# One multiply of the VectorE exponential handed to GpSimd in a conformer block, with the whole order planned again

## The chip, the cores and the metric

The kernel runs on one core of a Trainium2 chip. A core has five engines that run side by side, each with its own fixed list of instructions, and that wait for each other by semaphores: TensorE (PE in the profile; its weight loads are listed apart as PEld), VectorE (DVE), ScalarE (ACT), GpSimd (POOL) and SyncE (SP, which here only issues transfers). Data lie in SBUF, or in PSUM, where TensorE writes. The metric is the device time of one execution in microseconds; before the change it is 914.84 us (median of 3 runs, 914.69 to 915.0).

## The reference, cut to what matters

A conformer block on x of shape (2, 4000, 144) in bf16: a feed-forward layer, self-attention over 4000 tokens with 4 heads of 36, a gated convolution of width 5, a second feed-forward layer and a last normalization.

```python
h = _layernorm(x);  h = _silu(h @ w_ff1a) @ w_ff1b;  x = x + 0.5 * h
h = _layernorm(x);  qkv = h @ w_qkv                      # q, k, v: (2, 4, 4000, 36)
scores = jnp.einsum('bhqd,bhkd->bhqk', q, k) * Dh ** (-0.5)
p = _softmax(scores, axis=-1)
att = jnp.einsum('bhqk,bhkd->bhqd', p, v)
x = x + att @ w_o
h = _layernorm(x) @ w_pw1;  h = a * _sigmoid(b)          # a, b: the halves of h
c = sum over i of hp[:, i:i + T, :] * dw[i]              # hp: h padded by 2 at both ends
x = x + _silu(c) @ w_pw2
h = _layernorm(x);  h = _silu(h @ w_ff2a) @ w_ff2b;  x = x + 0.5 * h
return _layernorm(x)
```

The exponentials of the softmax are 2 x 4 x 4000 x 4000 = 128 million numbers, and they set the size of the work.

## The kernel before, in words

**Tiles.** The 8000 tokens are 16 chunks of 500 queries (8 for each batch). For one chunk the keys are taken 64 at a time: 62 full tiles and a rest of 32 keys. A tile is a pair of PSUM banks of 128 x 500: four matmuls of a 64-row corner of the array give the scores of 64 keys, 500 queries and 4 heads (`scores`, called by `emit_S`; in the profile PS<-QT,KT). The exponentials of a tile are written as bf16 to one of 11 buffers PT (128 x 1000), and four matmuls of PT against the values VA add them to the chunk's output in the two last banks (`emit_O` and `o_quads`; PS<-PT,VA). A column of ones among the values gives the softmax's sum.

**Two ways to an exponential.** Most tiles go to ScalarE: one ACTIVATE with Exp over both banks (`emit_exp`; ACT PT<-PS 128x1000). 167 of them go to VectorE (`dve_tile`, lines 1385 to 1416). The scores are scaled so that adding a bias and rounding to a 16-bit integer gives the bits of a bf16 power of two with a linear mantissa. VectorE does, for each tile z:

1. twice `tensor_scalar` from a PSUM bank to int16 in z (DVE PT<-PS, 128x500); each one gives a bank back,
2. `tensor_scalar` on the bits of z: the mantissa alone, put between a half and one, into a second buffer y (DVE PT<-PT, uint16),
3. `tensor_tensor`: y = z * y in bf16 (DVE PT<-PT, 128x1000 bf16; line 1409),
4. `tensor_scalar` on the bits of z in place: the exponent alone (DVE PT<-PT, uint16); it must come after step 3, which reads z.

y and z are both handed to the output matmuls, so that such a tile costs PE eight of them and not four.

**Other work.** While the attention runs, the layers before it for later chunks (`pre`) and those after it for earlier chunks (`post1`, `post2`) are done in the gaps of all engines. Normalization (`ln`, lines 704 to 743): VectorE takes the statistics (ST), GpSimd computes the variance's inverse root with a power (RS<-RS,NHALF) and, outside the first and last part of the run, also the mean with its sign (RS<-ST) and four normalizing steps per chunk (XN<-X,RS, 125x144). GpSimd also copies the columns at the edge of a chunk for the convolution (U<-U).

**What sets the order.** Nothing is decided on the chip. `Rec` records every operation, keeps an estimated time for each engine (`R.free`), and at the end writes each engine's list with the semaphores needed (`replay`; all instructions are issued on its line 170, so in the profile all have line 170 and are told apart by their tiles). `Rec.op` reckons an operation's start from its engine, its operands and `cost`, for instance `c_act(n)`, `c_dve(n, rate)`, XN_COST, and SWITCH for a change of the kind of matmul on PE. Background work is written as generators that say what they need next (`need`). `pick_any` chooses the next one by estimated times and by rules with numbers from the tables POLICY, TJ and FJ; POLICY has one entry per 21 tiles of the attention. `due` decides if the next tile goes to VectorE: not more than LIVE such tiles at once, DGAP us at least between two, and only if VectorE's estimated time is not later than PE's plus DSLACK. The estimate knows engines, buffers and banks; it holds an operation's cost to be the same whatever other engines do at the time. In the first part (`mode["front"]`, until the keys of the first batch are there) and in the last one other rules hold.

Of the kernel before, what the change touches and what calls it, by code (L numbers as in the profile page):

```python
# [6 lines left out]
ALU = mybir.AluOpType  # L7
# [16 lines left out]
CH = 500  # L24
# [14 lines left out]
def c_dve(n, rate=1.0):  # L39
    return n / (960 * rate) + 0.07  # L40


def c_act(n):
    return n / 1200 + 0.051
# [6 lines left out]
class Rec:  # L51
# [6 lines left out]
    SWITCH = 0.095  # L58
# [12 lines left out]
    def op(self, eng, name, *a, r=(), w=(), q=None, cost=0.1, kind=None, lat=None, **k):  # L71
        o = Op()
# [18 lines left out]
        if eng == "pe" and self.filler is not None and not self.filling:  # L91
# [5 lines left out]
            start = self.free[eng]  # L97
# [3 lines left out]
        if eng == "pe":  # L101
            if kind != self.kind:
                start += self.SWITCH
            self.kind = kind
# [147 lines left out]
class Thread:  # L252
    def __init__(self, gen, ready, rank, no=0):
        self.no = no
        self.gen, self.ready, self.live, self.rank = gen, ready, True, rank
        self.req = None
# [67 lines left out]
def bass_standalone__conformer_family_zipformer__speech_kernel(  # L324
# [28 lines left out]
    def sb(name, shape, dt=BF16):  # L353
# [7 lines left out]
        0.0, -0.6, 0, 0.0, -0.3, 0.0, 0.0, 0.0, 0.0, -0.6, 0.15, 0.15, -0.6, 0.0, 0.15, 0,  # L361
        0.0, 0.0, 0.0, 0.0, 0.0, 0.0, 0.3, 0.6, 0.6, -0.3, -0.3, 0.0, 0.0, 0.0, 0.0, 0.0,
        0.0, 0.0, 0.0, 0.15, 0.0, 0.0, 0.0, -0.15, 0.0, 0.0, 0.0, 0.0, 0, 0.6, 0.0, 0.0,
    )
    FJ = (
        0.0, 0.0, 0.0, 0.0, 0.0, 0.0, 0.0, 0.0, 0.0, 0.0, 0.0, 0.0, 0.0, 0.0, 0.0, 0.0,
        0.0, 0.0, 0.0, 0.0, 0.0, 0.0, 0.0, 0.0, 0.0, 0.0, 0.0, 0.0, 0, 0.0, 0.0, 0.0,
        -0.25, 0.0, 0.0, 0.0, 0.0, 0.0, 0.0, 0.0, 0.0, 0.0, 0, 0.0, 0.0, 0.0, 0.0, 0.0,
        0.0, 0.0, 0.0, 0.0, 0.0, 0.0, 0.0, 0.0, 0.0, 0.0, 0.0, 0.0, 0.0, 0.0, 0.0, 0.0,
    )  # L370
    FLEX = 0.3
    SEG = 21
    POLICY = {
        "AHEAD": (
            0.56, 0.56, 0.56, 0.85, 0.85, 0.85, 0.56, 0.56, 0.56, 0.56, 0.56, 0.56, 1.0, 1.0, 0.56, 0.56,
            0.56, 0.56, 0.56, 0.56, 0.56, 0.56, 0.56, 0.56, 0.56, 0.6, 0.6, 0.5, 0.5, 0.5, 0.5, 0.56,
            0.56, 0.56, 0.56, 0.56, 0.56, 0.56, 0.56, 0.56, 0.5, 0.5, 0.56, 0.56, 0.56, 0.56, 0.56, 0.56,
# [3 lines left out]
            0.4, 0.4, 0.4, 2.5, 1.5, 1.5, 1.5, 1.0, 1.0, 1.5, 0.8, 0.4, 0.4, 0.4, 0.2, 0.2,  # L381
            0.4, 0.4, 0.4, 0.4, 1.5, 1.5, 1.5, 1.5, 4.0, 4.0, 4.0, 0.4, 0.4, 0.2, 0.4, 0.4,
            0.4, 0.4, 0.4, 0.4, 0.4, 0.4, 0.2, 0.2, 0.2, 0.4, 0.4, 0.4, 0.4, 1.5, 1.5, 1.5,
# [3 lines left out]
            2.0, 2.0, 4.0, 3.5, 4.5, 4.5, 4.5, 2.5, 2.5, 2.5, 2.5, 2.5, 2.5, 2.5, 2.5, 2.5,  # L387
            2.5, 2.5, 2.5, 2.5, 4.5, 2.5, 2.5, 2.5, 2.5, 2.5, 3.0, 3.25, 3.25, 3.0, 6.0, 3.25,
            3.25, 3.25, 3.25, 3.25, 4.0, 2.5, 2.5, 2.5, 3.25, 3.25, 3.25, 4.5, 4.5, 4.5, 3.25, 3.25,
# [3 lines left out]
            3, 3, 1, 1, 4, 4, 1, 1, 1, 3, 0, 0, 0, 0, 1, 1,  # L393
            1, 1, 1, 1, 1, 1, 1, 1, 1, 1, 1, 2, 1, 1, 1, 1,
            1, 1, 1, 1, 1, 1, 0, 0, 0, 0, 0, 1, 2, 0, 0, 1,
# [3 lines left out]
            1, 1, 2, 1, 1, 1, 1, 1, 1, 1, 1, 1, 1, 1, 1, 1,  # L399
            1, 1, 1, 1, 1, 1, 1, 1, 0, 2, 2, 2, 2, 2, 2, 1,  # L400
            1, 1, 1, 1, 1, 1, 2, 1, 1, 1, 1, 1, 1, 1, 3, 2,
            2,
        ),
        "LATE": (
            0.3, 0.3, 0.3, 0.3, 0.6, 0.6, 0.1, 0.2, 0.2, 0.2, 0.2, 0.2, 0.6, 0.6, 0.6, 0.1,
            0.1, 0.1, 0.1, 0.1, 0.1, 0.3, 0.3, 0.3, 0.3, 0.3, 0.2, 0.2, 0.2, 0.3, 0.3, 0.3,
            0.3, 0.3, 0.2, 0.2, 0.2, 0.2, 0.2, 0.2, 0.2, 0.2, 0.2, 0.2, 0.2, 0.2, 0.2, 0.2,
# [3 lines left out]
            1.8, 1.8, 1.6, 1.6, 1.6, 1.6, 1.6, 2.0, 2.5, 2.5, 2.5, 2.5, 2.5, 1.4, 2.5, 2.5,  # L411
            2.5, 1.8, 2.5, 2.5, 2.5, 1.6, 1.6, 1.6, 1.6, 1.6, 1.6, 1.4, 1.4, 1.4, 1.4, 3.5,
            3.5, 3.5, 3.5, 2.5, 2.5, 1.4, 1.4, 1.4, 1.6, 1.6, 3.0, 3.0, 1.4, 1.4, 1.4, 1.8,
# [3 lines left out]
            2, 2, 2, 2, 2, 2, 2, 2, 2, 3, 3, 3, 3, 3, 2, 2,  # L417
            5, 5, 4, 2, 2, 3, 2, 2, 2, 2, 2, 2, 2, 4, 2, 4,
            4, 5, 5, 2, 2, 2, 4, 5, 5, 5, 5, 5, 5, 5, 5, 4,
            3,  # L420
        ),
        "LIVE": (
            3, 3, 2, 2, 1, 1, 1, 1, 1, 2, 2, 2, 2, 3, 3, 3,
            3, 2, 2, 2, 2, 3, 3, 2, 2, 1, 1, 2, 2, 3, 3, 3,
            3, 3, 3, 3, 3, 3, 2, 3, 3, 4, 3, 3, 3, 3, 3, 3,
# [3 lines left out]
            2, 2, 3, 3, 1, 1, 3, 2, 1, 1, 1, 1, 1, 1, 3, 2,  # L429
            3, 3, 2, 2, 1, 2, 2, 2, 2, 1, 1, 2, 2, 2, 2, 2,  # L430
            2, 2, 2, 2, 2, 2, 3, 1, 1, 1, 3, 3, 3, 3, 3, 3,
            3,
        ),
        "EARLY": (
            2, 2, 2, 1, 3, 3, 2, 2, 2, 2, 2, 2, 2, 1, 1, 1,
            2, 2, 1, 1, 2, 2, 2, 2, 2, 2, 2, 2, 2, 2, 2, 2,
            2, 1, 1, 2, 2, 2, 3, 3, 3, 3, 3, 3, 2, 2, 2, 2,
            2,
        ),
        "PW": (  # L440
            0.12, 0.12, 0.12, 0.12, 0.05, 0.05, 0.3, 0.12, 0.12, 0.05, 0.05, 0.05, 0.05, 0.05, 0.12, 0.12,
            0.12, 0.12, 0.12, 0.12, 0.12, 0.12, 0.12, 0.12, 0.12, 0.12, 0.12, 0.12, 0.2, 0.2, 0.2, 0.12,
            0.3, 0.2, 0.2, 0.2, 0.2, 0.2, 0.12, 0.12, 0.12, 0.12, 0.12, 0.12, 0.12, 0.12, 0.12, 0.12,
# [3 lines left out]
            0.1, 0.1, 0.1, 0.1, 0.1, 0.1, 0.1, 0.1, 0.1, 0.1, 0.1, 0.1, 0.1, 0.1, 0.1, 0.1,  # L447
            0.1, 0.1, 0.1, 0.1, 0.1, 0.1, 0.1, 0.1, 0.0, 0.0, 0.0, 0.1, 0.1, 0.1, 0.1, 0.1,
            0.1, 0.1, 0.1, 0.1, 0.1, 0.1, 0.1, 0.1, 0.1, 0.1, 0.1, 0.1, 0.1, 0.1, 0.1, 0.1,
            0.1,  # L450
        ),
        "BGPICK": (
            0, 0, 0, 0, 0, 0, 0, 0, 0, 0, 0, 0, 0, 0, 0, 0,
            0, 0, 0, 0, 0, 0, 0, 0, 0, 0, 0, 0, 0, 0, 0, 0,
            1, 1, 1, 0, 0, 0, 1, 0, 0, 0, 0, 0, 0, 0, 0, 0,
# [3 lines left out]
            2, 2, 2, 1, 2, 2, 2, 2, 2, 0, 0, 0, 0, 0, 2, 2,  # L459
            2, 2, 2, 2, 2, 2, 2, 2, 2, 2, 2, 2, 2, 2, 0, 0,  # L460
# [4 lines left out]
            5, 5, 5, 5, 5, 5, 5, 5, 5, 5, 5, 5, 4, 4, 4, 5,  # L465
            5, 3, 3, 3, 3, 5, 5, 5, 5, 5, 5, 5, 5, 2, 2, 5,
            5, 5, 5, 5, 5, 5, 5, 5, 5, 5, 5, 5, 5, 1, 5, 5,
            5,
        ),
        "PRELAG": (  # L470
            0.7, 0.7, 0.7, 0.7, 0.7, 1.0, 0.7, 1.5, 1.5, 0.7, 0.7, 0.7, 0.7, 0.7, 0.7, 0.7,
            0.7, 0.7, 0.7, 0.7, 0.7, 0.7, 0.7, 0.7, 0.7, 0.7, 0.7, 1.0, 1.0, 1.0, 1.0, 0.7,
            0.7, 0.5, 0.5, 0.5, 0.5, 0.5, 0.7, 0.3, 0.3, 0.3, 0.7, 0.7, 0.5, 0.5, 0.5, 0.5,
            1.0,
        ),
        "LAGD": (
            1, 1, 1, 1, 1, 1, 1, 0, 0, 0, 0, 0, 1, 1, 0, 1,
            1, 1, 1, 1, 1, 1, 1, 1, 1, 1, 1, 1, 1, 0, 0, 0,
            1, 1, 1, 1, 1, 1, 1, 1, 1, 1, 1, 0, 0, 0, 0, 1,
# [147 lines left out]
    def now(k):  # L627
        return POLICY[k][seg[0]]

# [74 lines left out]
    def ln(c, bs, e=False):  # L704
# [15 lines left out]
        if not calm:  # L720
            op("pool", "tensor_scalar", RS[0:rows, u, 2, 0:n], ST[0:rows, u, 0:n, 1], -1.0, None, op0=ALU.mult,
               r=[("MV", u)], w=[("NM", u)], cost=0.3)
            for j in range(n):
                op("pool", "tensor_scalar", XN[0:rows, u, j, :], X[0:rows, c * NB + b0 + j, :], RS[0:rows, u, 2, j:j + 1],
                   RS[0:rows, u, 0, j:j + 1], op0=ALU.add, op1=ALU.mult,
                   r=[("X", c, b0 + j), ("NM", u), ("RS", u)] + xe, w=[("XN", u)], cost=XN_COST, lat=XN_LAT)
# [18 lines left out]
    XN_COST = 0.65  # L745
    XN_LAT = 0.6
    POW_COST = 1.22
# [596 lines left out]
    def scores(n, hh, bk, cost):  # L1344
        _, c, t = its[n]
        b = c // CPB
        k0, q0 = t * KT_ROWS, c * CH
        kcs = {min(k0 // CH, CPB - 1), min((k0 + KT_ROWS - 1) // CH, CPB - 1)}
        for p in range(2):
            op("pe", "matmul", PSV[64 * p:64 * p + 64, bk, 0:CH],  # L1350
               lhsT=KT[64 * hh:64 * hh + 64, p, b, k0:k0 + KT_ROWS], rhs=QT[64 * hh:64 * hh + 64, p, q0:q0 + CH],
               start=True, stop=True, skip_group_check=True,
               r=([("WKT", 0, "a")] if b == 0 and k0 + KT_ROWS <= 2 * TB else [("WKT", b * CPB + kc) for kc in kcs])
               + [("WQT", c)], w=[("ps", bk)], cost=cost, kind="q",
               lat=0.36 if cost < 0.1 else 0.31)
# [29 lines left out]
    def dve_tile(n):  # L1385
        z = None
        for hh in range(2):
# [20 lines left out]
        yield need("dve")  # L1408
        op("dve", "tensor_tensor", yf, zf, yf, op=ALU.mult, r=[("PT", z), ("PT", y)], w=[("PT", y)],
           cost=c_dve(2 * CH, 2), kind="e")  # L1410
# [5 lines left out]
        live_dve[0] -= 1  # L1416

# [3 lines left out]
    def o_quads(m, p, cost):  # L1421
# [12 lines left out]
        for hh in range(2):  # L1434
            op("pe", "matmul", PSV[64 * hh:64 * hh + DH + 1, BX + p, 0:CH],
               lhsT=VA[64 * p:64 * p + 64, blk, hh, 0:DH + 1], rhs=PT[64 * p:64 * p + 64, pt, hh, :],
               r=[("PT", pt), ("VA", cc), "VA1"], w=[("ps", BX + p)], cost=cost, kind="q", lat=0.33, **flags)
# [86 lines left out]
    def pick_any():  # L1524
# [46 lines left out]
        if n_s[0] >= NIT and o:  # L1571
            return o[0]
        left = len(ptp.free) - owed[0]
# [132 lines left out]
```

## Time and profile before

| | |
|---|---|
| runs, median (lowest to highest) | 914.84 us (914.69 to 915.0) |
| the profiled execution | 914.9 us |
| its span, first to last instruction | 913.1 us |
| granted TensorE clock | 0.999 |
| busy: PE, DVE, ACT, POOL | 890.1, 802.0, 872.9, 277.5 us |
| first and last full exponential on ACT start | 20.6 and some 877 us |
| XN steps on GpSimd | 224, 131.8 us |
| DVE exponential tiles | 167 |

Busy time is the time in which at least one instruction of the engine runs. ACT's instructions overlap at their ends, so that the mean of one (1050 ns for an exponential) is longer than what one adds to the busy time (777.2 / 841 = 0.924 us). A wait is put down to the engine and tile that ended it. In a row of a group the last part is the idle time of the engine just before that group's instructions. PE's busy time includes the pipeline of matmuls and does not tell how full PE is; its waits do.

### The profile page before, as it was taken

To read this page: it belongs to the slowest core of one execution; us is meant where nothing else is said; L and a number is where in the kernel's file an instruction comes from. 1 tells how busy PE (TensorE), PEld (TensorE's weight loads), DVE (VectorE), ACT (ScalarE), POOL (GpSimd) and SP (SyncE) were. 2 spreads that over 40 slices of the span, in tenths; PEclk is the share of its full clock that TensorE was granted. 3 is DMA by queue.
4 is the path that set the end of the run, shared out by engine and by line. 5 is a ranking of instruction groups with operands and counts; after the bars stand their busy time and mean duration, and the time that the engine had idled before them with its cause. 6 is when DMAs were issued, how large, how long until landed. Compare 5 with 4: busy or idle time off the path is not lost.

```text
span 913.1 us, 27439 instructions
## 1 busy us (share of the span) xinstructions
PE 890.1 (97%) x11946; PEld 411.2 (45%) x11946; DVE 802.0 (88%) x1756; ACT 872.9 (96%) x1105; POOL 277.5 (30%) x519
## 2 busy tenths in 40 slices
PE   8999999999999999999999999999999999999996
PEld 7544434444444444444444444444434344444455
DVE  8988898898989999898988799897889699978987
ACT  5899999999999999999999999999999999999984
POOL 5121041145111612223415333240605050403143
PEclk9999999999999999999999999999999999999999
DMA  4000000000000000000000000000000000000000
GB/s 114 34 2 1 2 2 1 1 3 1 3 3 1 3 2 2 2 3 1 2 2 14 1 9 8 8 2 1 15 1 2 8 9 2 8 1 8 2 8 26
DMA packets 7322, 7.36 MB, mean 8 GB/s; under 512 B 2376, under 2 KB 7202, under 8 KB 7202
## 3 DMA queue, kind: packets, MB, share of 16 engines
q1 hardware_dynamic: 5786, 5.00, 1.8%
q8 instruction: 93, 1.52, 0.7%
q10 hardware_dynamic: 1416, 0.62, 0.3%
q14 instruction: 27, 0.22, 0.1%
HBM read 3.31 MB, written 2.30 MB: 6 GB/s over the span
## 4 chain that ended last, share of the span: by engine, by line
ACT 51%; PE 43%; DVE 4%; issue 1%; DMA 0%; POOL 0%; POOLq 0%; DVEq 0%
ACT PT L170 46%; PE PS L170 43%; ACT TH L170 5%; DVE HT L170 1%; DVE PT L170 1%; DVE ST L170 1%; DMA X<-in_x_dram 0%; DVE X L170 0%; DVE XN L170 0%; DVE QT L170 0%; POOL RS L170 0%; DVE XT L170 0%; DVE RS L170 0%; DVE SW L170 0%; DVE VA L170 0%
## 5 line engine op out<-in xcount | busy, mean ns | idle before, releaser
L170 ACT ACTIVATE PT<-PS 128x1000 bf16<-128x1000 f32 (+1 forms) x841 | 777.2, 1050 | 8.3 <-PE PS L170 5.9
L170 PE MATMUL PS<-QT,KT 64*64 64x500 bf16 x3968 | 415.6, 383 | 8.6 <-ACT PT L170 5.6
L170 PE MATMUL PS<-PT,VA 64*37 64x500 bf16 x4636 | 396.1, 373 | 1.9 <-DVE QT L170 1.4
L170 DVE TENSOR_SCALAR PT<-PS 128x500 int16<-128x500 f32 x334 | 222.4, 671 | 31.5 <-PE PS L170 29.5
L170 PEld LDWEIGHTS PS<-QT,KT 64*64 64x64 bf16 x3968 | 123.8, 104 | 195.7 <-ACT PT L170 112.5
L170 PEld LDWEIGHTS PS<-PT,VA 64*37 64x37 bf16 x4636 | 132.1, 95 | 111.3 <-issue 26.7
L170 POOL TENSOR_SCALAR RS<-ST 125x4 f32<-125x4 f32 x112 | 36.6, 327 | 471.0 <-DVE ST L170 465.8
L170 DVE TENSOR_SCALAR PT<-PT 128x1000 uint16<-128x1000 uint16 x334 | 134.7, 416 | 1.3
L170 POOL TENSOR_SCALAR XN<-X,RS 125x144 bf16<-125x144 bf16 x224 | 131.8, 599 | 5.8
L170 POOL TENSOR_TENSOR RS<-RS,NHALF 125x4 f32<-125x4 f32 (+2 forms) x101 | 94.1, 936 | 101.6 <-DVE RS L170 96.9
L170 DVE TENSOR_TENSOR PT<-PT 128x1000 bf16<-128x1000 bf16 x167 | 113.0, 681 | 1.5
L170 ACT ACTIVATE TH<-PS 128x500 bf16<-128x500 f32 (+3 forms) x198 | 104.3, 552 | 6.7 <-PE PS L170 5.6
L170 DVE SCALAR_TENSOR_TENSOR HT<-TH,PS 128x500 bf16<-128x500 bf16 (+1 forms) x135 | 80.6, 616 | 25.1 <-ACT TH L170 24.4
L170 PE MATMUL PS<-XT,WA 72*128 72x500 bf16 (+2 forms) x280 | 74.3, 360 | 0.6 <-DVE VA L170 0.3
L170 DVE SCALAR_TENSOR_TENSOR X<-PS,X 125x288 bf16<-125x288 f32 x128 | 57.4, 452 | 14.8 <-PE PS L170 13.1
L170 DVE BATCH_NORM_STATS2 ST<-X 125x6 f32<-125x288 bf16 (+1 forms) x160 | 65.8, 447 | 1.0 <-DMA X<-in_x_dram 0.8
L170 PE MATMUL PS<-WB,HT 128*125 128x144 bf16 (+1 forms) x640 | 52.7, 230 | 0.3 <-DVE HT L170 0.3
L170 PEld LDWEIGHTS PS<-WB,HT 128*125 128x125 bf16 (+1 forms) x640 | 44.3, 136 | 14.8 <-issue 3.8
L170 PE MATMUL PS<-IDENT,XN 125*72 125x125 bf16 x512 | 42.4, 221 | 1.5 <-DVE XN L170 0.9
L170 DVE COPY XT<-PS 72x1000 bf16<-72x1000 bf16 (+2 forms) x65 | 39.9, 617 | 3.3 <-PE PS L170 2.5
L170 PEld LDWEIGHTS PS<-IDENT,XN 125*72 125x72 bf16 x512 | 31.5, 112 | 20.2 <-issue 12.6
L170 PE MATMUL PS<-U,DG 128*128 128x250 bf16 (+5 forms) x204 | 34.3, 265 | 0.1
(86 smaller groups left out, 560.6 us busy)
## 6 DMA issues: line engine op xcount, KB each, us to landing
X<-in_x_dram SPq DMA_DIRECT2D x16, 140.6 KB
out_dram<-XN SPq DMA_DIRECT2D x14, 140.6 KB
WA<-in_w_ff1a_dram ACTq DMA_DIRECT2D x1, 144.0 KB
WB<-in_w_ff1b_dram ACTq DMA_DIRECT2D x1, 144.0 KB, 2.6
WA<-in_w_ff2a_dram SPq DMA_DIRECT2D x1, 144.0 KB
WB<-in_w_ff2b_dram SPq DMA_DIRECT2D x1, 144.0 KB
out_dram<-XN SPq DMA_DIRECT2D x2, 70.3 KB
WQKV<-in_w_qkv_dram ACTq DMA_DIRECT2D x1, 121.5 KB
```

Of the source, the lines that this page charges most:

```text
L170: ins = getattr(eng, o.name)(*o.a, **o.k)
```

## The change

In `dve_tile`, step 3 is issued on GpSimd if the plan holds it to be free early enough, and on VectorE otherwise or in the first part. G_COST is what the plan reckons for it. This comes about for 115 of now 171 tiles. Buffers and dependencies are the same: y is written by GpSimd, PE's matmuls on y and VectorE's step 4 on z wait for it.

The planner's estimates are changed in a few places: `c_act`, SWITCH, an extra time (`bub`) for the first matmul of a score or output group after a switch or a wait, and the normalizing steps on GpSimd (0.45 us each and 0.8 more for the first, in place of 0.65 each). Its rule for the next matmul can hold background work back for a while (BURST, BAGE). All tables are new, and with them the order of the instructions on every engine.

```diff
 def c_act(n):
-    return n / 1200 + 0.051
+    return n / 1200 + 0.053
...
-    SWITCH = 0.095
+    SWITCH = 0.094
...
             if kind != self.kind:
-                start += self.SWITCH
+                start += self.SWITCH + bub[0] + (0.006 if self.kind == "q" else 0.0)
+            elif start > self.free["pe"] + 0.01:
+                start += bub[1]
...
     POLICY = {
+        "PTS": (
+            0.5, 0.5, 0.5, 0.5, 0.5, 0.5, 0.5, 0.5, 0.5, 0.5, 0.5, 0.5, 0.5, 0.5, 0.5, 0.5,
...
         "DGAP": (
-            2.0, 2.0, 4.0, 3.5, 4.5, 4.5, 4.5, 2.5, 2.5, 2.5, 2.5, 2.5, 2.5, 2.5, 2.5, 2.5,
...
+            2.0, 2.0, 4.0, 3.5, 4.5, 4.5, 4.5, 4.5, 2.5, 2.5, 2.5, 2.5, 4.5, 2.5, 2.5, 2.5,
+            2.5, 2.5, 2.5, 2.5, 2.0, 2.0, 2.0, 2.0, 2.5, 2.5, 2.5, 3.0, 1.5, 1.5, 1.5, 1.5,
...
         "LIVE": (
+            3, 3, 2, 2, 2, 1, 1, 1, 1, 1, 1, 1, 1, 3, 3, 3,
+            3, 2, 3, 4, 4, 3, 1, 3, 3, 3, 3, 3, 3, 3, 3, 3,
+            3, 3, 3, 3, 3, 3, 2, 3, 3, 3, 3, 3, 3, 3, 3, 3,
             3,
         ),
...
-                   r=[("X", c, b0 + j), ("NM", u), ("RS", u)] + xe, w=[("XN", u)], cost=XN_COST, lat=XN_LAT)
+                   r=[("X", c, b0 + j), ("NM", u), ("RS", u)] + xe, w=[("XN", u)], cost=XN_COST + (j == 0) * XN_FIRST, lat=XN_LAT)
...
-    XN_COST = 0.65
+    XN_COST = 0.45
     XN_LAT = 0.6
+    XN_FIRST = 0.8
...
-        yield need("dve")
-        op("dve", "tensor_tensor", yf, zf, yf, op=ALU.mult, r=[("PT", z), ("PT", y)], w=[("PT", y)],
-           cost=c_dve(2 * CH, 2), kind="e")
+        pool = not mode["front"] and R.free["pool"] < R.free["dve"] + now("PTS")
+        yield need("pool" if pool else "dve")
+        op("pool" if pool else "dve", "tensor_tensor", yf, zf, yf, op=ALU.mult, r=[("PT", z), ("PT", y)], w=[("PT", y)],
+           cost=G_COST if pool else c_dve(2 * CH, 2), kind="e")
...
+    G_COST = 2.3
...
+        for q in ok:
+            if q[2].seen is not q[2].req:
+                q[2].seen, q[2].since = q[2].req, R.free["pe"]
+        if ok and R.kind == "q" and (s or o) and sum(q[2].req.dur for q in ok) < now("BURST") and min(
+                q[2].since for q in ok) > R.free["pe"] - now("BAGE"):
+            ok = []
```

## The prediction

> **What bounds the kernel now.** I read the page first (engine shares, then the slices, then the chain), next the busy time by stretch, the waits of the middle of the run, and last the rows of the two engines that the change touches. The profiled execution took 914.9 us, of which 913.1 is span and 1.8 lies around it; the median of the runs is 914.84, so a difference to the one is a difference to the other.
>
> ```profile
> PE 890.1 (97%) x11946; PEld 411.2 (45%) x11946; DVE 802.0 (88%) x1756; ACT 872.9 (96%) x1105; POOL 277.5 (30%) x519
> ...
> ACT 51%; PE 43%; DVE 4%; issue 1%; DMA 0%; POOL 0%; POOLq 0%; DVEq 0%
> ...
> L170 ACT ACTIVATE PT<-PS 128x1000 bf16<-128x1000 f32 (+1 forms) x841 | 777.2, 1050 | 8.3 <-PE PS L170 5.9
> L170 DVE TENSOR_SCALAR PT<-PS 128x500 int16<-128x500 f32 x334 | 222.4, 671 | 31.5 <-PE PS L170 29.5
> L170 DVE TENSOR_SCALAR PT<-PT 128x1000 uint16<-128x1000 uint16 x334 | 134.7, 416 | 1.3
> L170 POOL TENSOR_SCALAR XN<-X,RS 125x144 bf16<-125x144 bf16 x224 | 131.8, 599 | 5.8
> L170 DVE TENSOR_TENSOR PT<-PT 128x1000 bf16<-128x1000 bf16 x167 | 113.0, 681 | 1.5
> ```
>
> The chain is ACT and PE by turns; VectorE has 4% of it and GpSimd nothing. By stretch (first column the length, then PE, weight loads, DVE, ACT, POOL):
>
> ```profile
> 0.00:47.00 47.00, 43.49 (x496) 29.74 (x497) 40.83 (x125) 32.52 (x61) 15.91 (x35) 1.00 0.25 72
> 47.00:126.00 79.00, 77.89 (x1086) 32.73 (x1084) 67.18 (x172) 77.08 (x94) 12.32 (x19) 1.00 0.01 2
> 126.00:486.00 360.00, 357.20 (x4918) 158.26 (x4916) 328.83 (x676) 355.22 (x431) 111.63 (x207) 1.00 0.01 2
> 486.00:850.00 364.00, 356.24 (x4757) 156.08 (x4754) 313.88 (x643) 361.84 (x450) 118.43 (x227) 1.00 0.02 6
> ```
>
> From 126 to 850 us ACT works 717.1 of 724 us. That is the bound: only 6.9 us are left to squeeze there without taking work off ACT. It is also fragile. The waits of that same stretch:
>
> ```profile
> PEld PS L170 <- ACT PT L170: 102.8, 280, 1.1
> ...
> PEld PS L170 <- DVE PT L170: 56.0, 195, 0.6
> ```
>
> PE waits for ACT 0.37 us at a time (102.8/280); that is all the lead it has when VectorE is late. And it already waits for VectorE's exponential tiles 195 times, just in time. The order of every engine is fixed ahead, so a late VectorE instruction holds all that stands behind it.
>
> **The part that decides: two engines on one path to SBUF.** GpSimd's normalizing step XN takes 451 ns at least, 461 in the middle, but up to 2267:
>
> ```profile
> L170 POOL TENSOR_SCALAR XN<-X,RS x216: 451/461/2267, 125.8 to 846.9; 125x144 bf16<-125x144 bf16 x108
> ...
> 302.85 2.27 POOL L170 TENSOR_SCALAR XN<-X,RS 125x144 bf16<-125x144 bf16 x1
> ...
> 302.95 0.74 DVE L170 TENSOR_SCALAR PT<-PT 128x1000 uint16<-128x1000 uint16 x2
> 303.61 1.26 DVE L170 TENSOR_TENSOR PT<-PT 128x1000 bf16<-128x1000 bf16 x2
> ```
>
> The 2.27 us one stood still while VectorE ran four SBUF-to-SBUF steps on PT. Taken over the trace, the 122 XN steps that meet no PT<-PT step average 459 ns and none is over 466, whatever else VectorE does; the 102 that meet one average 768. The other way round, VectorE's PT<-PT tensor_scalar takes 410 ns where GpSimd is idle and 443 on average, 646 at most, on its 66 meetings with an XN; the multiply goes from 671 to 713 on 40 meetings, 831 at most. So the two exclude each other: here GpSimd lost 102 x 0.31 = 32 us by it, and VectorE 66 x 0.033 + 40 x 0.042 = 3.9 us, because an XN is short.
>
> **The change part by part.** *Four exponentials more leave ACT* (171 VectorE tiles for 167): 4 x 0.924 us (777.2/841) = -3.7 us on the bound. For them VectorE does 4 x (2 x 0.666 + 2 x 0.403) = 8.6 us more, without multiplies, and PE four more passes of PT against VA, 16 matmuls at 396.1/4636 = 0.085 us, 1.4 us beside ACT. *115 multiplies leave VectorE*: 115 x 0.677 = 77.9 us, on an engine that is not the bound; by itself worth nothing but the waits for it, which are limited to the 6.9 us of ACT's idle time. I count 0 and keep -4 as the end.
>
> *115 multiplies come to GpSimd.* The trace has none of this size. From RS<-ST (4 elements, 194 ns at least) and XN (144 elements, 451 ns), one element costs 257/140 = 1.84 ns, so 1000 elements cost 2.0 us with one input read and up to 3.9 us if the second is read after the first. The plan reckons with 2.3, near the lower end, where I stay. GpSimd goes from 277.5 to about 542 us, 59%. Behind a multiply stand the next normalization (56 groups) and the halo copies; PE waited on GpSimd's RS 4 times for 1.4 us in all in the middle, and GpSimd itself waits 433.9 us for ST there: background work with room, 0. If that room were gone, half of the 56 groups 1.15 us late would be 32 us on the background chain. No DMA is added, and SP's order of stores does not pass anything that matters (16 stores in all).
>
> *The added waits.* The exponent step of the same tile (z in place) may run only when GpSimd has read z, some 1.6 us later than now; the plan knows this and puts other work between. y is ready 1.6 us later, too, and PE's pass waits for it in the plan's reckoning; 11 PT buffers stay. What the plan does not know is the exclusion. In the trace 77 other-tile PT<-PT steps start within 2.3 us of the 167 multiplies (229 in all, less one own step per multiply where there is one), 0.46 each; for 115 that makes 53 meetings. A VectorE step that comes while a 2.1 us stream runs waits 1.05 us in the mean if GpSimd keeps the path for the whole stream: 56 us. If it lets go as quickly as with XN, it is 53 x 0.04 = 2 us. For XN itself the same reckoning (106 meetings, half of the time streaming, half of 0.25 us) gives 7 us where 3.9 were seen; that share makes 31 us here, 0.6 us per meeting. PE's lead hides 0.37 of each, which leaves 53 x 0.23 = 12 us. The ends are 0 and 53 x (1.05 - 0.37) = 36 us. I take 12: the row is of the same pair of engines. GpSimd's own lateness (VectorE is in PT<-PT steps for 232 of the 724 us now, 78 less then, 21%; 0.3 us for each meeting) stays under PE's 0.37.
>
> The Trainium skill (SBUF — State Buffer, Who interferes with whom) says that whoever of the two starts first keeps the shared ports for the whole instruction. The trace bears that out only in part: 33 tensor_scalar steps begin inside GpSimd's power step, which lasts 1.04 us or more, and none takes over 420 ns. With the whole 2.3 us held, a meeting would cost 1.15 us and the sum would be 53 x (1.15 - 0.37) = 41 us instead of 12.
>
> ```profile
> 279.38 1.04 POOL L170 TENSOR_TENSOR RS<-RS,NHALF 125x4 f32<-125x4 f32 x1
> ...
> 279.67 0.41 DVE L170 TENSOR_SCALAR PT<-PT 128x1000 uint16<-128x1000 uint16 x1
> ```
>
> *The new tables, the picking rule and the planner's constants* emit no instruction; they reorder all of them. Up to 126 us the multiply stays on VectorE, so only the order differs there; ACT is idle 16.4 us in that part (126 - 32.5 - 77.1) and 16 of the last 34.6 us. Either could move by a fifth, 3 us, up or down. I take 0.
>
> Sum: 914.9 - 3.7 + 12 = 923.2, rounded up for the multiplies that PE meets late: **924 us**.
>
> **The rivals.** *The relief holds (faster).* The place is VectorE's queue between 126 and 850 us: 78 us of freed time swallow the blocked steps before PE or ACT sees them, or GpSimd yields. ACT loses its four exponentials and perhaps half of its 6.9 us of idle time and a little of the ends: 914.9 - 3.7 - 3.4 = 908. For it: with 31 us of blocks against 69 us net freed, VectorE is still less loaded than now, and the trace shows GpSimd losing eight times as much as VectorE. Against: PE's lead is a third of a microsecond, and a block comes in one lump. It decides below 3.7/53 = 0.07 us lost on ACT per meeting. *The multiply is much longer than planned (slower still).* At 3.9 us, y is 1.6 us late 115 times; PE waited just in time on 195 of 616 VectorE tile events in the middle (154 tiles, two bank releases and two outputs each), so 115 x 0.32 x (1.6 - 0.37) = 45 us: 914.9 - 3.7 + 12 + 45 = 968. For it: two inputs. Against: nothing but the plan's own 2.3. *Nothing that can be told.* Blocks of 0.07 us per meeting just eat the four exponentials: 915.
>
> The Trainium skill (GPSIMD Engine Reference, Elementwise — side-by-side cycle accounting) has 4497 ns for a two-input add of 2048 elements, from which I would estimate 2.2 us; no run here shows it yet, and by it the sum above stays as it is.
>
> **How the numbers follow.** A difference under 0.2% (1.8 us) is about what a measurement of this kernel cannot tell from none. Blocks that reach ACT: 0.48, its own range 917 to 941 (1 to 26 us beyond the middle's gain). Relief holds: 0.36, 903 to 912. No difference: 0.07. Long multiply: 0.09. The range runs from 905 (leaving 0.08 of the relief's chance below) to 943 (leaving the long multiply and a little of the first case above). Faster 0.36, same 0.07, slower 0.57.
>
> **What would show it.** Right: GpSimd's multiply is a row of 115 with a middle of 2.2 to 2.6 us; PT<-PT steps on VectorE that took 410 ns now show a maximum near 2 us and a mean clearly over 443; ACT's row still ends its waits on PE PS, but its idle time from 126 to 850 us is some 15 to 25 us instead of 6.9; PE's waits on DVE PT are longer at the longest than 0.6 us. Wrong: the maximum of VectorE's PT<-PT stays under 700 ns (GpSimd yields), ACT's idle time stays under 7 us and the time falls with four full exponentials fewer (825 now, by the row of that shape); or the multiply's row is at 3 us and more, and PE waits on POOL PT. It would also be wrong if the ends of the run, outside 126 to 850 us, moved by over 3 us.

## The result and the profile after

The changed kernel takes 942.33 us (median of 4 runs, 941.25 to 942.63) against 914.82 (914.69 to 915.0): a ratio of 1.0298, with a 95% interval of 1.0281 to 1.0316. It is slower, as forecast, but by 27.5 us where 9 were forecast. The profiled execution took 942.2 us, 940.3 of them span.

The page of the changed kernel (engine shares, chain, and three groups: busy time and mean, then idle time ahead and who ended it):

```profile
PE 900.7 (96%) x11992; PEld 416.2 (44%) x11992; DVE 788.1 (84%) x1661; ACT 875.2 (93%) x1102; POOL 516.7 (55%) x640
...
PE 58%; ACT 23%; DVE 17%; issue 1%; POOL 1%; DMA 0%; ACTq 0%; DVEq 0%
...
L172 ACT ACTIVATE PT<-PS 128x1000 bf16<-128x1000 f32 x837 | 778.8, 1029 | 30.9 <-PE PS L172 26.2
...
L172 POOL TENSOR_TENSOR PT<-PT 128x1000 bf16<-128x1000 bf16 x115 | 242.9, 2113 | 236.9 <-DVE PT L172 236.8
...
L172 DVE TENSOR_SCALAR PT<-PT 128x1000 uint16<-128x1000 uint16 x342 | 171.1, 511 | 6.4 <-POOL PT L172 4.0
```

VectorE is less busy than before (788.1 us for 802.0), and yet its share of the chain has gone from 4% to 17%: it holds the others up for longer, although it is less loaded. Of the 78 us that the multiplies took off it, its bit steps on PT (the two `tensor_scalar` on the bits) took back 33 by growing from 416 to 511 ns (342 x 0.511 - 334 x 0.416 = 36, 3 of that for eight steps more). ACT's exponentials, four fewer, stood waiting for 30.9 us in place of 8.3.

By stretch (length, then PE, weight loads, DVE, ACT, POOL):

```profile
126.00:486.00 360.00, 350.29 (x4725) 154.37 (x4723) 304.63 (x596) 342.32 (x416) 212.32 (x261) 1.00 0.01 3
486.00:850.00 364.00, 348.23 (x4684) 152.64 (x4683) 307.17 (x594) 352.29 (x433) 218.52 (x249) 1.00 0.02 5
```

In these 724 us ACT works 694.6, so that it is idle 29.4 us where it was 6.9. The waits of the same stretch (total, times, longest):

```profile
PEld PS L172 <- DVE PT L172: 79.5, 206, 1.7
PEld PS L172 <- ACT PT L172: 70.1, 202, 0.8
...
ACT PT L172 <- PE PS L172: 23.0, 39, 1.9
```

PE waits for VectorE's tiles about as often as before (206 times for 195), but up to 1.7 us and not 0.6, and ACT waits for PE 23.0 us where in the kernel before it was

```profile
ACT PT L170 <- PE PS L170: 3.9, 14, 0.6
```

The rows of the instructions on PT, minimum, median and maximum in ns, tell why. On VectorE, before and after:

```profile
L170 DVE TENSOR_SCALAR PT<-PT x334: 358/410/646, 87.5 to 874.4; 128x1000 uint16<-128x1000 uint16 x167
...
L172 DVE TENSOR_SCALAR PT<-PT x342: 366/412/2279, 111.7 to 907.3; 128x1000 uint16<-128x1000 uint16 x171
```

and on GpSimd, after:

```profile
L172 POOL TENSOR_TENSOR PT<-PT x115: 2068/2078/2919, 126.4 to 905.2; 128x1000 bf16<-128x1000 bf16 x115
```

The bit step's median is what it was, its maximum 2279 ns, in place of 646. Worked out over the trace: 53 bit steps overlap a GpSimd multiply and take 1026 ns on average, 32.6 us in all above the 411 that the others take in the middle. Nearly all of this lies with 30 of them that are held, 1.09 us each: they begin inside a multiply that has more than 0.2 us to go, and every one of them ends 0.28 us (0.275 to 0.280) after it, however long that is. The 64 multiplies that meet no such step take 2.07 to 2.10 us, the 51 others 2.16 on average. So this time it is VectorE that loses. One case, from the timelines of the four engines (start, length, what, and the idle time ahead):

```profile
597.81 4.22 POOL L172 TENSOR_TENSOR PT<-PT 128x1000 bf16<-128x1000 bf16 x2 [3.54 <-DVE PT L172]
...
600.03 2.27 DVE L172 TENSOR_SCALAR PT<-PT 128x1000 uint16<-128x1000 uint16 x1 [0.53 <-POOL PT L172]
...
602.36 0.12 PEld L172 LDWEIGHTS PS<-PT,VA 64*37 64x37 bf16 x6 [1.14 <-DVE PT L172]
...
603.21 1.90 ACT L172 ACTIVATE PT<-PS 128x1000 bf16<-128x1000 f32 x2 [1.30 <-PE PS L172]
```

GpSimd runs two multiplies one after the other. The first has released a bit step, which begins just as the second starts to stream, and takes 2.27 us for 0.41. PE, which has its output matmuls in front of the next scores, waits 1.14 us; ACT then has nothing for 1.30 us. In all, ACT's idle stretches that begin within 4 us after the end of one of the 30 held steps sum to 17 of the 30.4 us that it is idle from 126 us to its last exponential, in 116 of these 782 us.

### The profile page after: what moved, and what is told of

Read it like the earlier page. It is cut to its first block, busy times and chain, and to the rows that moved or that the text cites. A ratio compares the mean times of both kernels' runs of the same rounds, so it can differ in the third digit from the quotient of the medians.

```text
span 940.3 us, 27550 instructions
## 1 busy us (share of the span) xinstructions
PE 900.7 (96%) x11992; PEld 416.2 (44%) x11992; DVE 788.1 (84%) x1661; ACT 875.2 (93%) x1102; POOL 516.7 (55%) x640
## 4 chain that ended last, share of the span: by engine, by line
PE 58%; ACT 23%; DVE 17%; issue 1%; POOL 1%; DMA 0%; ACTq 0%; DVEq 0%
PE PS L172 58%; ACT PT L172 20%; DVE PT L172 10%; ACT TH L172 2%; DVE ST L172 1%; DVE HT L172 1%; DVE X L172 1%; DVE XT L172 1%; DVE XN L172 1%; DVE QT L172 1%; POOL PT L172 1%; DMA X<-in_x_dram 0%; DVE AN L172 0%; POOL RS L172 0%; DVE RS L172 0%
## 5 line engine op out<-in xcount | busy, mean ns | idle before, releaser
L172 ACT ACTIVATE PT<-PS 128x1000 bf16<-128x1000 f32 x837 | 778.8, 1029 | 30.9 <-PE PS L172 26.2
L172 PE MATMUL PS<-PT,VA 64*37 64x500 bf16 x4652 | 410.8, 375 | 16.2 <-DVE PT L172 13.8
L172 POOL TENSOR_TENSOR PT<-PT 128x1000 bf16<-128x1000 bf16 x115 | 242.9, 2113 | 236.9 <-DVE PT L172 236.8
L172 DVE TENSOR_SCALAR PT<-PS 128x500 int16<-128x500 f32 x342 | 229.0, 672 | 49.7 <-PE PS L172 46.6
L172 DVE TENSOR_SCALAR PT<-PT 128x1000 uint16<-128x1000 uint16 x342 | 171.1, 511 | 6.4 <-POOL PT L172 4.0
L172 POOL TENSOR_SCALAR XN<-X,RS 125x144 bf16<-125x144 bf16 x228 | 128.6, 575 | 5.9
L172 DVE SCALAR_TENSOR_TENSOR HT<-TH,PS 128x500 bf16<-128x500 bf16 (+1 forms) x140 | 84.2, 617 | 21.9 <-ACT TH L172 21.2
L172 DVE SCALAR_TENSOR_TENSOR X<-PS,X 125x288 bf16<-125x288 f32 (+1 forms) x128 | 57.1, 452 | 16.6 <-PE PS L172 15.5
L172 DVE COPY XT<-PS 72x1000 bf16<-72x1000 bf16 (+1 forms) x65 | 40.0, 617 | 8.1 <-PE PS L172 7.4
L172 DVE TENSOR_TENSOR PT<-PT 128x1000 bf16<-128x1000 bf16 x56 | 38.7, 692 | 0.7
```

The costliest lines, as they stand in the source:

```text
L172: ins = getattr(eng, o.name)(*o.a, **o.k)
```

## The experiments

All of them keep the order of every engine's list as one of the two kernels has it: the edit is made after the planning, and only the instructions named change or move. The edits are shown shortened, with words in place of loops. They are given with the time of the kernel before on the same chip (914.89 us for the first four, 914.97 for the others).

### No stream on GpSimd, everything else in its place

```diff
+    for o in R.ops:
+        if is_mult(o):                      # a multiply on GpSimd, 115 times
+            two times: o.deps + scratch; tensor_tensor(GS[0:TB, n], GS[0:TB, 100], NHALF, op=ALU.pow)
```

> The changed kernel with every instruction in its place, but each of the 115 GpSimd multiplies is replaced by two power steps on 125x4 numbers of a scratch tile (1.04 us each in the trace of before, so 2.1 us as the multiply's 2.08), with the same waits and the same waiters. The multiply of these tiles is left out. Theory of the blocks (VectorE's bit steps on PT stand still while GpSimd streams): the bit steps come back to about 415 ns on average, none over 700, ACT's idle time from 126 us to the last exponential falls from 29 to under 12 us, and the time is 917 to 923 us. Rival, the order: the newly planned order itself is the worse one, the bit steps recover but the time stays at 935 us or more. Rival, GpSimd's lateness: PE and VectorE wait for y, which comes as late here as there; the time stays at 935 us or more, and waits on GpSimd's result grow or stay.

Measured: 919.96 us (919.66 to 920.08), ratio 1.0055 [1.004, 1.007]. The bit steps and the waits from 126 to 850 us:

```profile
L172 DVE TENSOR_SCALAR PT<-PT x342: 364/412/627, 111.6 to 885.2; 128x1000 uint16<-128x1000 uint16 x171
```

```profile
PEld PS L172 <- DVE PT L172: 53.1, 181, 0.6
```

The mean of the bit steps is 417 ns, the longest 627, and PE's waits for VectorE are those of the kernel before. GpSimd is about as long at work for each tile (1.99 us in the middle for the two power steps, 2.08 for the multiply), with the same waits, and only does not stream the tile through SBUF: 56 bit steps overlap a power step and take 413 ns on average, 440 at most. So 942.33 - 919.96 = 22.4 us of the change's 27.5 are the blocks. ACT's idle time from 126 us to the last exponential is 12.2 us (30.4 in the changed kernel), where under 12 was expected. The 5.1 us that remain belong to something else, although the four exponentials are gone from ACT here, too.

### The stream cut into four

```diff
+            for i in range(4):
+                tensor_tensor(*(v[:, i * 250:(i + 1) * 250] for v in (yf, zf, yf)), op=ALU.mult)
```

> The changed kernel in the same order, with each GpSimd multiply cut into four of 250 columns. Theory of the blocks, with the path free between two instructions: a bit step waits for the rest of one piece, 0.55 us at most, 0.25 on average, so that most waits are short of PE's lead; the longest bit step is about 1.0 us, ACT's idle time about halves, and the time is 922 to 930 us, although the four pieces last longer together (some 2.4 us). If GpSimd keeps the path from piece to piece, bit steps of 2 us stay, and so does the time, 940 to 948 us. Theory of GpSimd's lateness: it finishes later, so over 942 us.

Measured: 933.23 us (933.17 to 933.27), ratio 1.0201 [1.0185, 1.0216]. On VectorE and on GpSimd:

```profile
L172 DVE TENSOR_SCALAR PT<-PT x342: 366/415/876, 111.5 to 898.8; 128x1000 uint16<-128x1000 uint16 x171
```

```profile
L172 POOL TENSOR_TENSOR PT<-PT x460: 647/658/1487, 126.2 to 898.1; 128x250 bf16<-128x250 bf16 x154
...
  PEld PS L172: 20.6, 38
  DVE PT L172: 19.6, 30
```

The longest bit step falls from 2279 to 876 ns: the path is let go between two instructions. What the steps over 600 ns cost VectorE falls from 32.9 to 11.2 us. But the whole multiply is longer (2.51 us in the middle) and is now broken into by VectorE (pieces up to 1.49 us), and the last two lines, who waited for it, were 4.7 and 4.0 us in the changed kernel. So 9 us are won, less than expected (922 to 930 us): by these waits, a part of the blocks has turned into lateness of GpSimd.

### The multiply back on VectorE, in the new order

```diff
+        if is_mult(o):
+            o.eng = "dve"
```

> The changed kernel in the same order, with the 115 multiplies issued on VectorE at their places in the order: nothing streams on GpSimd, and VectorE does 115 x 0.68 = 78 us more than planned there. Theory of the blocks, and VectorE's freed time worth little: 78 us in steps of 0.68 us, where 33 us in steps of 1.06 us were lost to waits; 920 to 935 us, below the changed kernel. If the order leans on the freed time: 945 us or more. If the order is what costs: about 940 us.

Measured: 938.52 us (938.43 to 938.69), ratio 1.0259 [1.0243, 1.0274]. No bit step is longer than 624 ns, and PE's waits for VectorE's tiles over the whole run are as long in sum as with the blocks (86.6 us there):

```profile
PEld PS L172 <- DVE PT L172: 85.9, 248, 1.1
```

That is more than the theory of the blocks gave (920 to 935), and near the 940 that was put down for an order that costs by itself. For an order that leans on the freed time 945 or more had been put down. So this run alone does not tell the two apart. The run without a stream does: the same order, with the multiply on neither engine, takes 919.96 us, so that the 115 x 0.68 us put back cost 938.52 - 919.96 = 18.6 us, 0.16 us each. The new order leans on the time that it has freed. It also follows that, of the two kernels that do all the work in this order, the one with the multiplies on GpSimd is only 942.33 - 938.52 = 3.8 us slower: the 22.4 us are the price of the blocks against no multiply at all, not against the multiply on VectorE.

### The price of a block by itself: 31 delays in the kernel before

```diff
+        if id(o) in late:                   # 31 bit steps, evenly spread
+            three times: bn_stats(LS[0:TB, i, :], LB[0:TB, :, :])   # scratch, on VectorE
```

> The kernel before in its own order, with 31 delays of some 1.1 us put into VectorE's queue, each ahead of a bit step on PT between 126 us and the end: three statistics steps on a scratch tile, 447 ns each by their row and some 0.37 us from start to start. Nothing on GpSimd is changed. This is the price of a block by itself; the changed kernel had 31 bit steps over 600 ns, 32.9 us more than normal together. The prediction's reckoning by the mean (0.23 of 0.6 us reaches ACT) gives 34 x 0.38 = 13 us, 928 us. The same lead of 0.37 us taken off each delay gives 31 x 0.73 = 23 us, 938 us. No lead at all: 949 us. All hidden by VectorE's idle time: 915 to 918 us.

Measured: 938.44 us (938.33 to 938.51), ratio 1.0258 [1.024, 1.0275]. One of the delays in VectorE's timeline:

```profile
146.64 1.17 DVE L170 BATCH_NORM_STATS2 LS<-LB 125x6 f32<-125x288 bf16 x3
147.73 0.40 DVE L170 TENSOR_SCALAR PT<-PT 128x1000 uint16<-128x1000 uint16 x1
```

The bit step begins 1.09 us later. GpSimd is left alone here, and the kernel before is made as slow as the changed one by the delays alone: 23.5 us for 31 x 1.09 = 34 us, 0.76 us for each. The 31 steps over 600 ns from which the number of delays was taken are 29 of the 30 held ones and 2 that an XN held. The 938 us that come from taking the lead off each delay are met; the 928 us that come from the mean are not.

### The same delay, three times as fine

```diff
-            three times: bn_stats(...)      # at 31 bit steps
+            once: bn_stats(...)             # at 93 bit steps
```

> The kernel before in its own order, with the same 34 us of delay in VectorE's queue as in the run with 31 delays, cut three times as fine: 93 single statistics steps (some 0.37 us each) ahead of 93 bit steps. If PE's lead of about 0.37 us covers a delay of that size, as the prediction's subtraction has it, the time is 915 to 918 us. If there is no lead, and only the sum counts, it is what 31 lumps cost, 935 to 942 us. In between, with the lead there at some times only: 920 to 932 us.

Measured: 927.65 us (927.58 to 927.75), ratio 1.0139 [1.0123, 1.0154]: 12.7 us, 0.14 us for each delay of 0.37, between the two theories. So PE's lead is real, but it is not the 0.37 us of its mean at every place: a delay as long as the mean lead still costs 0.14. The 30 held steps of the changed kernel lose 1.09 us each on average, as much as one of the 31 lumps. At the lumps' price they cost 30 x 0.76 = 22.8 us, where the run without a stream has 22.4. This is an estimate, since the prices come from the order of the kernel before.

### GpSimd's part halved

```diff
-            two times: tensor_tensor(..., op=ALU.pow)
+            once: tensor_tensor(..., op=ALU.pow)
```

> The changed kernel's order with one power step (1.04 us) on scratch in place of each GpSimd multiply, where the run without a stream had two; the multiply of these tiles is left out. It tells if the 5.1 us by which that run stayed above the kernel before are GpSimd's lateness (y and the freeing of z 2.1 us after the bit step) or the order itself. Lateness: 915 to 917.5 us. The order itself: 919 to 920.5 us.

Measured: 919.28 us (918.83 to 919.38), ratio 1.0046 [1.0031, 1.0061]. To halve GpSimd's time per tile is worth 0.7 us; 4.3 us more than before remain, with an order that has four exponentials fewer on ACT. If the other half were worth as much, 3.6 us would be left to the order itself.

### VectorE freed of the multiply, in the order before

```diff
+    for i in range(115):
+        mults[i * len(mults) // 115].a = (LB[:, i % 30, :], LB[:, 30, :], LB[:, 31, :])   # 8 columns of scratch
```

> The kernel before in its own order, with 115 of its 154 VectorE multiplies after 126 us shrunk to 8 columns of a scratch tile, some 0.6 us less each: VectorE is freed of about 70 us and GpSimd does nothing for it. The multiply of these tiles is left out. This is the most that taking the multiply off VectorE can give in that order. The prediction counted 0, with -4 as the end: 911 to 915 us. If VectorE's load were what bounds: under 908 us.

Measured: 914.82 us (914.36 to 915.24), ratio 0.9998 [0.9988, 1.0007]. By stretch, DVE in the third place and ACT in the fourth after the length:

```profile
126.00:486.00 360.00, 357.15 (x4918) 158.12 (x4916) 305.88 (x677) 355.21 (x431) 100.07 (x207) 1.00 0.01 2
486.00:850.00 364.00, 355.69 (x4757) 155.75 (x4754) 290.02 (x642) 361.84 (x450) 105.95 (x227) 1.00 0.02 6
```

VectorE is busy 595.9 us of the 724, 47 less than before (642.7), and ACT's 717.05 are what they were. That is less than the 70 expected to be freed, but with these 47 us gone the time has not moved: in the order before, an engine that took over these multiplies could win nothing by it.

### The multiplies that were met back on VectorE

```diff
+    met = (0, 19, 21, 27, 32, 34, 37, 39, 43, 44, 45, 51, 53, 54, 59, 61, 63, 65, 66, 70, 71, 78, 80, 82, 83, 90, 96, 99, 108)
+    for i in met:
+        mults[i].eng = "dve"
```

> The changed kernel in its order, with the 29 multiplies during whose streams VectorE stood still in the changed kernel's trace issued on VectorE; the other 86 stay on GpSimd. Theory of the blocks: the long bit steps go (a few new ones may come, since the times shift), and 29 x 0.68 us come to VectorE, which by the run with all 115 on VectorE (18.6 us more than with no stream, 0.16 each) cost some 5 us: 923 to 929 us. If the blocks were spread over all multiplies and not these: above 935 us.

Measured: 926.06 us (925.91 to 926.19), ratio 1.0121 [1.0106, 1.0136]. The bit steps:

```profile
L172 DVE TENSOR_SCALAR PT<-PT x342: 363/411/840, 111.7 to 891.2; 128x1000 uint16<-128x1000 uint16 x171
```

A quarter of the multiplies held three quarters of the loss (942.33 - 926.06 = 16.3 of 22.4 us). What is left to the run without a stream, 6.1 us, is near the 29 x 0.161 = 4.7 that the moved multiplies cost on VectorE. It is the quickest of the kernels that do all the work in the new order, and still 11 us behind the kernel before.

## Why the prediction was right or wrong

**The bound, and what freed time is worth** (right). ACT was the bound, and the 78 us taken off VectorE were counted at 0: with VectorE freed of 47 us and nothing else changed, the time is the same within 0.1%.

**The two engines on one path** (right in kind; that the numbers fit is in part luck). VectorE's bit steps stand still while GpSimd streams, as was forecast from how GpSimd's short steps held them. 53 meetings were forecast and 53 steps overlap a multiply; 31 us of waiting were forecast, and it is 32.6. But two misses cancel in this. The 53 forecast were steps that begin inside a stream. Only 38 do, and 30 of them are held; 5 begin in its last 0.1 us, 3 ran at once while the multiply was held (2.77 to 2.92 us), and the other 15 of the 53 were already running when the multiply began. And a held step does not lose 0.6 us, the share taken over from XN, but nearly all that is left of the stream, 1.09 us on average. That share was no sign that the path is let go early: in the trace of before, the 15 bit steps that were held by an XN with over 0.15 us to go all ended 0.27 us after it, too.

The multiply was put at 2.0 to 3.9 us by the rows and 2.3 by the plan, and it is 2.08, so that the rival of the long multiply fell. Of the signs named, this is below the 2.2 to 2.6 given for its middle, and ACT's idle time of 29.4 us from 126 to 850 us is above the 15 to 25.

**What of the waits reaches ACT** (wrong size: 12 us forecast, 22.4 measured). The step that failed is "PE's lead hides 0.37 of each, which leaves 53 x 0.23". It took the lead off the mean wait, 0.6 us. But 23 of the 53 meetings wait next to nothing and the other 30 some 1.09 us each, and a lead cannot be lent from the short to the long. Taken off each held step it leaves 30 x 0.72 = 22 us. The two runs with delays of known size show the same: 34 us cost 23.5 in 31 lumps and 12.7 in 93. The fit of the 22 us is again better than its reasoning, since the 0.37 is the mean of the 280 times that PE did wait for ACT, and the 93 delays of that size cost 0.14 us each and not nothing.

**The four exponentials and the new order** (wrong: -3.7 and 0 forecast, +5.1 measured together). The step that failed is to put the reordering at 0. Without the stream the changed order is 5.1 us slower than the old one, and still 4.3 with GpSimd's time per tile halved. ACT's idle time tells where: from the first exponential to 126 us 8.8 us for 6.9, from there to the last exponential 12.2 for 7.7, while the part after the last exponential is 2.7 us shorter. Nor is all of the 3.7 us seen in ACT's work, which is 1.6 us less in sum without the stream. Each of the moves at the ends is within the 3 us that were allowed for; the middle was not allowed for at all. Which of the new tables or estimates does it stays open: that most of the 5.1 us lies with the order follows from the two runs, what in it costs them is not shown.

**The rivals.** That the relief holds was decided by 0.07 us lost on ACT per meeting; it is 22.4/53 = 0.42. What would have shown it wrong, a longest bit step under 700 ns, did not come.

**The rules of the Trainium skill.** The rule of the Trainium skill that the first to start keeps the shared ports for the whole instruction (SBUF — State Buffer, Who interferes with whom) was held against the 1.04 us power steps. For the multiply the trace agrees: the 30 held steps end 0.28 us after it whatever was left of it, and the longest waited 1.87 us of a stream of 2.08. Cut into four, the longest is 876 ns with pieces of 658, so that it is the instruction that holds. For the power steps it does not show: with 230 of them in the multiplies' places, the bit steps average 417 ns. The sum by that rule, 41 us, was too high because it counted 53 held steps; with the 30 that were held it is 30 x (1.15 - 0.37) = 23 us. The 2.2 us that I estimated from the Trainium skill (GPSIMD Engine Reference, Elementwise — side-by-side cycle accounting) are near the 2.08 measured.

## What to carry to other kernels

Work moved to an engine that shares a path with its old owner has two prices, its own time and the standing still of the owner, and the owner is late at places that the plan did not choose; look in the trace for steps whose maximum is far from their median, and price the long ones one by one, not their mean. Time freed on an engine that is not the bound is worth nothing until the order uses it, and an order that has used it must be sure of it. If a shared path cannot be avoided, short instructions hold it for a shorter time, at a higher sum.

## What the runs showed of the hardware

GpSimd's bf16 multiply of 128x1000 with two inputs takes 2.07 to 2.10 us undisturbed and 0.65 to 0.67 us for 250 columns. While it runs, VectorE's SBUF-to-SBUF tensor_scalar on 16-bit numbers stands still, 1.87 us at the longest; if it begins with over 0.2 us of the multiply to go, it ends 0.28 us after it (30 steps), unless the multiply is the one held (3 steps). VectorE's steps that read PSUM do not stand still, and neither do its statistics: the conversion from PSUM to int16 averages 673 ns on its 118 meetings with a multiply and 672 elsewhere, the copy of bf16 from PSUM 674 and 673, the statistics 447 and 447, the residual from PSUM and SBUF 453 and 452. That ACT's busy time rose by 2.3 us with four exponentials fewer had not been expected: instructions that stand apart lose the overlap at their ends. One exponential adds 778.8/837 = 0.930 us, before 0.924, although its mean length has fallen from 1050 to 1029 ns.
